# Routed attention with an ELU network: conversion order, query masks on ScalarE, row sums of ten blocks on TensorE, weight sums on VectorE

## The chip, the core and the metric

The kernel runs on one core of a Trainium2 chip. A core has TensorE (matrix products, PE in the profile; PEld is its loading of weights), VectorE (DVE), ScalarE (ACT), GpSimd (POOL) and a queue for transfers (SP). The metric is the time of the core on the device in microseconds, the median of several runs.

## The reference, cut to what matters

Attention over 4 batches, 8 heads, 768 positions of 64 values each. Queries and keys are each assigned to the nearest of 16 centroids of their head, and a query sees only the keys of its own centroid. The result goes through a two-layer network with an ELU between.

```python
q_assign = np.argmax(np.einsum('bhsd,hcd->bhsc', q_n, c_n), axis=-1)
k_assign = np.argmax(np.einsum('bhsd,hcd->bhsc', k_n, c_n), axis=-1)
mask = q_assign[:, :, :, None] == k_assign[:, :, None, :]
scores = scale * np.matmul(q, k.transpose(0, 1, 3, 2))
scores = np.where(mask, scores, -1000000000.0)
attn = softmax(scores)                      # written out in the reference
attn_out = np.matmul(attn, v)
# ... (B,H,S,D) -> x of (B*S, H*D) = 3072 x 512
h = x @ w_in                                # 512 x 2048
g = np.where(h > 0.0, h, np.exp(np.minimum(h, 0.0)) - 1.0)
out = g @ w_out                             # 2048 x 512
```

The two weight matrices arrive as 64-bit floating point numbers, everything else in 32 bits.

## The kernel before

**Converting the weights.** 32 pieces of 128x512 weights are brought in as pairs of 32-bit words (low, high) and turned into 32-bit numbers. A step handles three pieces in different states. "Splitting" takes the mantissa bits and the exponent bits out of the high word; in between, ScalarE rebuilds the exponent and GpSimd scales the mantissa; "joining" adds sign and low word, and GpSimd multiplies the two parts. The tile `ex` has three buffers.

```python
for n in range(len(pieces) + 2) if wide else ():
    if n < len(pieces):                                   # split piece n
        high = words[n][0][:, :, 1]
        e = exps[n] = loads.tile([P, WC], U32, name="ex", tag="ex", bufs=3)
        nc.vector.tensor_scalar(                                            # L244
            pieces[n][0].bitcast(U32), high, 0xFFFFF, None, op0=Alu.bitwise_and)
        nc.vector.tensor_scalar(e, high, 0x7FF00000, None, op0=Alu.bitwise_and)  # L247
    if 0 <= n - 1 < len(pieces):                          # convert piece n - 1
        to, ex = pieces[n - 1][0], exps[n - 1]
        nc.scalar.activation(ex, ex, Act.Relu, scale=8.0, bias=off)         # L250
        nc.gpsimd.tensor_scalar(                                            # L251
            to, to.bitcast(U32), 2.0**-20, 1.0, op0=Alu.mult, op1=Alu.add)
    if n > 1:                                             # join piece n - 2
        to, ex = pieces[n - 2][0], exps.pop(n - 2)
        w, place, limit = words.pop(n - 2)
        nc.vector.scalar_tensor_tensor(                                     # L257
            ex, w[:, :, 1], 0x80000000, ex, op0=Alu.bitwise_and, op1=Alu.bitwise_or)
        nc.vector.scalar_tensor_tensor(                                     # L260
            to, w[:, :, 0], 2.0**-52, to, op0=Alu.mult, op1=Alu.add)
        nc.gpsimd.tensor_tensor(to, to, ex.bitcast(F32), op=Alu.mult)       # L263
        places.append((place, limit))
        ask()                                             # load the next words
    yield
```

`weigh(k)` runs k of these steps. There are three in each of the first ten attention blocks, and one beside each step of the network until the ninth block.

**An attention block** is one pair of heads and a third (256) of the queries; there are 48, twelve to a batch. Scores of block n are made in three tiles of PSUM, each from products of q and k (L401) and, added to them, products of two small masks (L410), of which `qm` is the queries' one. It holds 0 where a query belongs to a centroid and -2^80 elsewhere; the exponential of that is 0.

```python
def masks(n):
    b, third, pr = blocks[n]
    qm[n] = route.tile([P, QS], BF16, name="qm", tag="qm", bufs=2)
    for e in range(2):
        rows = slice(64 * e, 64 * e + 64)
        m = big[rows, pr % 2 : pr % 2 + 1]
        nc.vector.tensor_scalar(                                            # L374
            qm[n][rows], hot[b, 0][rows, side(pr, e), ts(third, QS)],
            m, m, op0=Alu.mult, op1=Alu.subtract)

def scores(n):
    for u in range(NT // 2):              # three tiles
        s = banks()                       # one of three pairs of PSUM banks
        # ... products L401 and L410 into s
        p = pu[n, u] = probs.tile([P, 2, 2 * QS], F32, name="p", tag="p")
        nc.scalar.activation(p, s, Act.Exp, scale=SCALE)                    # L418
        if n < LAG + 3:                   # LAG = 7
            weigh(1)
```

The sums of the rows of `p` are a product with ones (L436) on TensorE. Where `sums` has run, VectorE has added the parts first, and 4 small matmul instructions are left of 24.

```python
def sums(n):
    to = osum[n] = work.tile([P, 2, 2 * QS], F32, name="psum", tag="psum", bufs=1)
    nc.vector.tensor_tensor(to, pu[n, 0], pu[n, 1], op=Alu.add)             # L424
    nc.vector.tensor_tensor(to, to, pu[n, 2], op=Alu.add)                   # L425
    nc.vector.tensor_tensor(to[:, :, :QS], to[:, :, :QS], to[:, :, QS:], op=Alu.add)  # L426

def values(n):
    # ... products of p and v into o_bank (L447); row sums into d (L436)
    nc.scalar.copy(x, o_bank[:, :QS])                                       # L461
    nc.scalar.activation(r, d[:, :QS], Act.Copy, accum_out=...)             # L463
    nc.vector.reciprocal(r, r)                                              # L464
    nc.gpsimd.tensor_tensor(x, x, r, op=Alu.mult)                           # L465
```

`check(n)` reads r once more on ScalarE (L471).

**The network** runs seven blocks behind, on a third of a batch's rows, in groups of steps: two hidden steps; two more; four products; three products. A hidden step is 32 products (L486, 64 instructions) into a bank pair, an exponential (ScalarE, L496), a clamp (GpSimd, L497), and one step later `elu` (VectorE, L503, then a difference, L505 or L507), which frees the bank pair. The products of the second layer (L516) use fewer multiplications by working with sums of `g` and of the weights. Those of the weights are made once, in two halves, after the last conversion:

```python
def sum_weights(half):
    of = slice(half * FC // 4, (half + 1) * FC // 4)
    e_, f_, g_, h_ = (x[:, of] for x in w_parts())     # views of w_out
    t1, t2, t4 = (w_sum[:, n, of] for n in range(3))
    nc.gpsimd.tensor_tensor(t1, f_, e_, op=Alu.subtract)                    # L295
    nc.gpsimd.tensor_tensor(f_, h_, f_, op=Alu.subtract)                    # L296
    nc.vector.tensor_tensor(t2, h_, t1, op=Alu.subtract)                    # L297
    nc.vector.tensor_tensor(t4, g_, t2, op=Alu.subtract)                    # L298
```

In the second layer `first` multiplies e_, `second` g_, `third_` the changed f_, `fourth` t4.

**The order of a block's iteration** (cut):

```python
for n in range(len(blocks) + LAG):
    if n <= len(blocks) and n > 0:
        values(n - 1)
    # ... loads of q, k, v
    if n + 1 < len(blocks) and at + 1 < NB:      # not the last block of a batch
        masks(n + 1)
    if n < len(blocks):
        scores(n)
    if 0 < n <= len(blocks):
        check(n - 1)
    if n < len(blocks):
        if n >= LAG:
            sums(n)
        # ... in the last four blocks of a batch: transposes of the next q, k (VectorE, L310)
    # in the last block of a batch, beside the network's steps: similarities (TensorE, L331)
    # and assignment (VectorE, L338 to L363) of the next queries, then of the next keys,
    # then masks(n + 1)
    if n == LAG + 2:
        weigh(100)
        for half in range(2):
            sum_weights(half)
    # the network's group n - LAG, step by step; one weigh(1) after each where n < LAG + 2
```

At the start the queries are transposed (ScalarE copies qT out of PSUM, L323), assigned, then `masks(0)`, and then the same for the keys (kT).

Of the kernel before, what the change touches and what calls it, by code (L numbers as in the profile page):

```python
# [9 lines left out]
F32 = mybir.dt.float32  # L10
# [3 lines left out]
Act = mybir.ActivationFunctionType  # L14
Alu = mybir.AluOpType
# [3 lines left out]
P = 128  # L19


BIG = float(2.0**80)
# [38 lines left out]
def main_path(ctx, tc, c, q, k, v, centroids, moe_w_in, moe_w_out, out):  # L61
    nc = tc.nc
# [16 lines left out]
    const = ctx.enter_context(tc.tile_pool(name="const", bufs=1))  # L79
# [81 lines left out]
    big = const.tile([P, 2], F32, name="big")  # L161
    for e in range(2):
        rows = slice(64 * e, 64 * e + 64)
        nc.vector.tensor_reduce(
            big[rows],
            ident[rows].rearrange("q (h x e c) -> q x e h c", h=2, x=2, e=2)[:, :, e],
            axis=Axis.XY,
            op=Alu.add,
        )
    nc.vector.tensor_scalar(big, big, BIG, None, op0=Alu.mult)  # L170

    sq = work.tile([P, D], F32, name="sq", tag="r", bufs=1)
# [15 lines left out]
    for e in range(2):  # L188
# [17 lines left out]
    pieces = [  # L206
        (w_in[:, ch, ts(g, WC)], moe_w_in[ts(ch, P), ts(g, WC)])
        for g in range(DF // WC)
        for ch in range(KC)
    ]  # L210
# [4 lines left out]
    words, exps = {}, {}  # L215
    places = []
    asked = 0

    def ask():

        nonlocal asked
        while asked < len(pieces):
            to, src = pieces[asked]
            if not wide:
                nc.sync.dma_start(to, src)
                asked += 1
                continue
            places[:] = [x for x in places if asked < x[1]]
            if not places:
                return  # L230
            place, limit = places.pop(0)
            w = place.bitcast(U32)
            nc.sync.dma_start(w, src.bitcast(U32))
            words[asked] = (w.rearrange("p (n w) -> p n w", w=2), place, limit)
            asked += 1

    def weight_steps():


        for n in range(len(pieces) + 2) if wide else ():  # L240
            if n < len(pieces):
                high = words[n][0][:, :, 1]
                e = exps[n] = loads.tile([P, WC], U32, name="ex", tag="ex", bufs=3)
                nc.vector.tensor_scalar(  # L244
                    pieces[n][0].bitcast(U32), high, 0xFFFFF, None, op0=Alu.bitwise_and
                )
                nc.vector.tensor_scalar(e, high, 0x7FF00000, None, op0=Alu.bitwise_and)  # L247
            if 0 <= n - 1 < len(pieces):
                to, ex = pieces[n - 1][0], exps[n - 1]
                nc.scalar.activation(ex, ex, Act.Relu, scale=8.0, bias=off)  # L250
                nc.gpsimd.tensor_scalar(  # L251
                    to, to.bitcast(U32), 2.0**-20, 1.0, op0=Alu.mult, op1=Alu.add
                )
            if n > 1:
                to, ex = pieces[n - 2][0], exps.pop(n - 2)
                w, place, limit = words.pop(n - 2)
                nc.vector.scalar_tensor_tensor(  # L257
                    ex, w[:, :, 1], 0x80000000, ex, op0=Alu.bitwise_and, op1=Alu.bitwise_or
                )
                nc.vector.scalar_tensor_tensor(  # L260
                    to, w[:, :, 0], 2.0**-52, to, op0=Alu.mult, op1=Alu.add
                )
                nc.gpsimd.tensor_tensor(to, to, ex.bitcast(F32), op=Alu.mult)  # L263
                places.append((place, limit))
                ask()
            yield

    spare = w_sum.rearrange("p a f m -> p (a f m)")
# [16 lines left out]
    def w_parts():  # L285
        e_, f_ = w_out[:, : FC // 2, :QS], w_out[:, : FC // 2, QS:]
        g_, h_ = w_out[:, FC // 2 :, :QS], w_out[:, FC // 2 :, QS:]
        return e_, f_, g_, h_

    def sum_weights(half):  # L290

        of = slice(half * FC // 4, (half + 1) * FC // 4)
        e_, f_, g_, h_ = (x[:, of] for x in w_parts())
        t1, t2, t4 = (w_sum[:, n, of] for n in range(3))
        nc.gpsimd.tensor_tensor(t1, f_, e_, op=Alu.subtract)  # L295
        nc.gpsimd.tensor_tensor(f_, h_, f_, op=Alu.subtract)  # L296
        nc.vector.tensor_tensor(t2, h_, t1, op=Alu.subtract)  # L297
        nc.vector.tensor_tensor(t4, g_, t2, op=Alu.subtract)  # L298
# [66 lines left out]
    def side(pr, e):  # L365
        return int(pr // 2 != e)
# [4 lines that stand above are left out]
        for e in range(2):  # L371
            rows = slice(64 * e, 64 * e + 64)
            m = big[rows, pr % 2 : pr % 2 + 1]
            nc.vector.tensor_scalar(  # L374
                qm[n][rows],
                hot[b, 0][rows, side(pr, e), ts(third, QS)],
                m,
                m,
                op0=Alu.mult,
                op1=Alu.subtract,  # L380
            )


    LAG = 7
# [43 lines left out]
    def values(n):  # L428

        b, third, pr = blocks[n]  # L430
        d = banks()[:, 0]
        summed = osum.pop(n, None)

        def row_sums(p, m, kt, last):
            for e in range(2):
                nc.tensor.matmul(  # L436
                    d[64 * e : 64 * e + 64, :QS],
                    lhsT=ones,
                    rhs=p[:, e, ts(m, QS)],
                    start=(kt == 0),  # L440
                    stop=(kt == last),
                )

        for kt in range(NT):
            p, m = pu[n, kt // 2], kt % 2
            for e in range(2):
                nc.tensor.matmul(  # L447
                    o_bank[64 * e : 64 * e + 64, :QS],
                    lhsT=raw["v", n][:, e, kt],
                    rhs=p[:, e, ts(m, QS)],  # L450
                    start=(kt == 0),
                    stop=(kt == NT - 1),
                )
            if summed is None:
                row_sums(p, m, kt, NT - 1)
        if summed is not None:
            row_sums(summed, 0, 0, 0)
        if pr == 0:
            xT[b, third] = xtp.tile([P, KC, QS], F32, name="xT", tag="xT")
        x = xT[b, third][:, pr]  # L460
        nc.scalar.copy(x, o_bank[:, :QS])  # L461
        r = work.tile([P, QS], F32, name="r", tag="r", bufs=1)
        nc.scalar.activation(r, d[:, :QS], Act.Copy, accum_out=d_sum[:, n : n + 1])  # L463
        nc.vector.reciprocal(r, r)  # L464
        nc.gpsimd.tensor_tensor(x, x, r, op=Alu.mult)  # L465
        rs[n] = r
# [154 lines left out]
    for n in range(len(blocks) + LAG):  # L621
        b, at = n // NB, n % NB
        ahead = b + 1 < B
        if n <= len(blocks) and n > 0:
            values(n - 1)
        if ahead:
            for pr in {5: [0], 6: [1], 9: [2], 10: [3]}.get(at, []):
                load("q", (b + 1) * NPR + pr)
                load("k", (b + 1) * NPR + pr)
        if n + 1 < len(blocks):  # L630
            load_v(n + 1)
        if n + 1 < len(blocks) and at + 1 < NB:
# [3 lines that stand above are left out]
        if 0 < n <= len(blocks):  # L636
            check(n - 1)
        if n < len(blocks):
            if n >= LAG:
                sums(n)  # L640
            if ahead and at in turns:
                for j in range(2):
                    turn((b + 1) * NPR + turns[at], j)
        beside = []
        if ahead and at + 1 == NB:
            beside.append(None)
            for j in range(2):
                beside.append(lambda b=b, j=j: [similar(b + 1, j, half) for half in range(2)])
                beside.append(lambda b=b, j=j: [assign(b + 1, j, half) for half in range(2)])
            beside.append(lambda n=n: masks(n + 1))  # L650
        main = groups[n - LAG] if n >= LAG else []
# [4 lines that stand above are left out]
        done = 0  # L656
        for m, step in enumerate(main):
            step()
            upto = len(beside) * (m + 1) // len(main)
            for other in beside[done:upto]:  # L660
                if other:
                    other()
            done = upto
            if n < LAG + 2:
                weigh(1)
        for other in beside[done:]:
            if other:
                other()
# [268 lines left out]
```

## Time and profile before

| | |
|---|---|
| Median of 3 runs | 1068.94 us (1066.64 to 1069.65) |
| Span of the profiled execution | 1066.4 us, clock 0.976 |
| Length of a block early on (45.67 to 57.73 us) | 12.06 us |
| Iterations 7, 8 and 9, from reciprocal to reciprocal | 105.99 to 130.22, to 161.74; the fourth product of the network ends at 191.9 us |
| Stage after that | 187 us to the end |
| Busy time of VectorE, ScalarE, GpSimd | 559.3, 293.8, 188.9 us |

The profile gives for each group of instructions its line in the kernel, its engine, what it writes and reads, its count, busy time and mean duration. Rows of a timeline start with the start time and the duration in us; a bracket at the end holds the idle time of the engine before the instruction and what ended it. Rows of waits give the waiting instruction, what it waited for, the total in us, how often, and the longest.

### The profile page before, as it was taken

The page shows a single profiled execution, that of the slowest core. Times are in us where ns is not written, and L with a number is a line of the kernel's source. Part 1 is how long each engine was busy: PE and PEld are TensorE (multiplying, and loading weights), DVE is VectorE, ACT ScalarE, POOL GpSimd, SP SyncE. Part 2 cuts the span into 40 slices and gives each one's busy share as a digit, 9 for nine tenths or more (in the row PEclk, how much of TensorE's full clock was granted, in tenths as well). Part 3 has the DMA queues.
Part 4 walks back from the last instruction along what each step waited for, and adds up shares of the span by engine and source line. Part 5 has one row for each costly group of instructions (what it writes and reads, how often), then busy time and mean ns, then how long its engine had stood idle before and what let it go on. Part 6 is the DMA issues. An engine that isn't in the chain of part 4 may idle for free.

```text
span 1066.4 us, 14860 instructions
## 1 busy us (share of the span) xinstructions
PE 1011.3 (95%) x6343; PEld 784.4 (74%) x6343; DVE 559.3 (52%) x740; ACT 293.8 (28%) x499; POOL 188.9 (18%) x195
## 2 busy tenths in 40 slices
PE   6988876999999999999999999999999999999996
PEld 4655654767877878877887887876787787788885
DVE  5778999476336336465534535656444534533131
ACT  3555331223123133122223223222322322321010
POOL 0555657011011011011011011011011011011010
PEclk9999886999999999999999999999999999999999
DMA  9628231100015012210013212210010000000000
GB/s 298 255 75 212 81 84 30 38 28 16 16 46 78 15 50 45 45 36 29 18 36 62 42 35 60 45 35 16 30 35 15 31 35 15 31 21 1 20 1 23
DMA packets 103961, 55.60 MB, mean 52 GB/s; under 512 B 83408, under 2 KB 96720, under 8 KB 103888
## 3 DMA queue, kind: packets, MB, share of 16 engines
q1 hardware_dynamic: 103888, 54.57, 18.8%
q8 instruction: 52, 0.85, 0.3%
q14 instruction: 21, 0.17, 0.0%
HBM read 48.27 MB, written 6.29 MB: 51 GB/s over the span
## 4 chain that ended last, share of the span: by engine, by line
PE 82%; DVE 13%; POOL 4%; issue 1%; DMA 0%; ACT 0%; DVEq 0%; POOLq 0%
PE banks L486 29%; PE f_bank L516 16%; PE o_bank L516 12%; PE banks L401 10%; PE o_bank L447 10%; PE banks L410 3%; DVE ex L257 2%; PE banks L436 2%; DVE r L464 1%; POOL w_in L263 1%; POOL w_out L263 1%; DVE ex L247 1%; DVE qm L374 1%; DVE w_in L260 1%; DVE w_out L260 1%; PE banks L331 1%
## 5 line engine op out<-in xcount | busy, mean ns | idle before, releaser
L486 PE MATMUL banks<-xT,w_in 128*128 128x256 f32 x1536 | 338.4, 381 | 0.3
L486 PEld LDWEIGHTS banks<-xT,w_in 128*128 128x128 f32 x1536 | 289.8, 190 | 47.8 <-ACT p L418 2.9
L401 PE MATMUL banks<-qT,kT 64*128 64x256 f32 x1152 | 174.5, 401 | 8.5 <-DVE gT L503 8.3
L418 ACT ACTIVATE p<-banks 128x1024 f32<-128x1024 f32 x144 | 147.3, 1023 | 58.6 <-PE banks L410 54.2
L447 PE MATMUL o_bank<-p,v_raw 128*64 128x256 f32 x1152 | 143.1, 387 | 11.6 <-ACT p L418 11.2
L464 DVE RECIPROCAL r<-r 128x256 f32<-128x256 f32 x48 | 84.0, 1749 | 113.7 <-ACT r L463 113.6
L503 DVE SCALAR_TENSOR_TENSOR gT<-gT,banks 128x1024 f32<-128x1024 f32 x48 | 58.4, 1216 | 156.8 <-POOL gT L497 156.7
L401 PEld LDWEIGHTS banks<-qT,kT 64*128 64x128 f32 x1152 | 91.7, 195 | 60.1 <-issue 11.3
L496 ACT ACTIVATE gT<-banks 128x1024 f32<-128x1024 f32 x48 | 49.1, 1024 | 280.9 <-PE banks L486 280.9
L447 PEld LDWEIGHTS o_bank<-p,v_raw 128*64 128x64 f32 x1152 | 78.9, 138 | 64.8 <-issue 17.2
L497 POOL TENSOR_SCALAR gT<-gT 128x1024 f32<-128x1024 f32 x48 | 52.8, 1100 | 320.0 <-ACT gT L496 320.0
L516 PE MATMUL o_bank<-w_out,gT 128*128 128x256 f32 x384 | 91.8, 393 | 8.1 <-POOL w_out L296 8.1
L465 POOL TENSOR_TENSOR xT<-xT,r 128x256 f32<-128x256 f32 x48 | 35.0, 729 | 318.7 <-DVE r L464 318.7
L410 PE MATMUL banks<-qm,hot 64*128 64x256 bf16 x576 | 82.9, 276 | 8.6 <-DVE qm L374 5.4
L516 PEld LDWEIGHTS o_bank<-w_out,gT 128*128 128x128 f32 x384 | 74.1, 196 | 22.5 <-POOL w_out L296 9.2
L516 PE MATMUL f_bank<-w_out,gT 128*128 128x256 f32 x384 | 87.1, 379 | 1.3 <-POOL w_out L263 1.3
L516 PEld LDWEIGHTS f_bank<-w_out,gT 128*128 128x128 f32 x384 | 72.9, 190 | 11.6 <-POOL w_out L263 1.7
L461 ACT COPY xT<-o_bank 128x256 f32<-128x256 f32 x48 | 17.8, 370 | 218.5 <-PE o_bank L447 218.4
L424 DVE TENSOR_TENSOR psum<-p 128x1024 f32<-128x1024 f32 x41 | 50.2, 1224 | 13.0 <-ACT p L418 12.7
L425 DVE TENSOR_TENSOR psum<-psum,p 128x1024 f32<-128x1024 f32 x41 | 52.9, 1290 | 5.0 <-ACT p L418 1.6
L516 PE MATMUL f_bank<-w_sum,g_sum 128*128 128x256 f32 x192 | 44.6, 386 | 1.2 <-DVE part L563 1.2
L374 DVE TENSOR_SCALAR qm<-hot,big 64x256 bf16<-64x256 bf16 x96 | 45.2, 470 | 1.0
(108 smaller groups left out, 829.2 us busy)
## 6 DMA issues: line engine op xcount, KB each, us to landing
v_raw<-in_v_dram SPq DMA_DIRECT2D x48, 384.0 KB, 3.2
w_sum<-in_moe_w_out_dram SPq DMA_DIRECT2D x12, 512.0 KB, 4.2
out_dram<-o_sb SPq DMA_DIRECT2D x24, 256.0 KB, 2.0
q_raw<-in_q_dram SPq DMA_DIRECT2D x48, 96.0 KB, 3.6
k_raw<-in_k_dram SPq DMA_DIRECT2D x48, 96.0 KB, 3.2
w_sum<-in_moe_w_in_dram SPq DMA_DIRECT2D x8, 512.0 KB, 6.6
w_out<-in_moe_w_in_dram SPq DMA_DIRECT2D x8, 512.0 KB, 10.4
w_out<-in_moe_w_out_dram SPq DMA_DIRECT2D x4, 512.0 KB, 4.3
```

Source lines behind the costliest of these rows:

```text
L374: nc.vector.tensor_scalar(qm[n][rows], hot[b, 0][rows, side(pr, e), ts(third, QS)], m, m, op0=Alu.mult, op1=Alu.subtract,)
L401: nc.tensor.matmul(s[:, e, ts(m, QS)], lhsT=T[i, 1][rows, ts(kt, P)], rhs=T[i, 0][rows, cols], start=True, stop=False,)
L410: nc.tensor.matmul(s[:, e, ts(m, QS)], lhsT=hot[b, 1][rows, side(pr, e), ts(kt, P)], rhs=qm[n][rows], start=False, stop=True,)
L418: nc.scalar.activation(p, s, Act.Exp, scale=SCALE)
L424: nc.vector.tensor_tensor(to, pu[n, 0], pu[n, 1], op=Alu.add)
L425: nc.vector.tensor_tensor(to, to, pu[n, 2], op=Alu.add)
L447: nc.tensor.matmul(o_bank[64 * e : 64 * e + 64, :QS], lhsT=raw["v", n][:, e, kt], rhs=p[:, e, ts(m, QS)], start=(kt == 0), stop=(kt == NT ...
L464: nc.vector.reciprocal(r, r)
L486: nc.tensor.matmul(hf[:, f], lhsT=w_in[:, ch, ts(4 * n + f, P)], rhs=xT[b, third][:, ch], start=(ch == 0 and f % 2 == 0), stop=(ch == KC - 1),
L497: nc.gpsimd.tensor_scalar(t, t, 1.0, 0.0, op0=Alu.min, op1=Alu.max)
L503: nc.vector.scalar_tensor_tensor(t, t, -1.0, hf, op0=Alu.add, op1=Alu.max)
L516: nc.tensor.matmul(to[:, :QS], lhsT=left[:, f], rhs=right[:, f], start=(f == 0), stop=(f == FC // 2 - 1),)
```

## The change

The conversion steps join piece n - 2 before they split piece n, so that the wait of the split for a buffer comes later. The masks of queries are made by ScalarE, as big * hot - big, with a new constant `minus`. In blocks 7, 8 and 9 VectorE no longer adds the parts of p, so TensorE sums the rows of ten blocks alone. Of the four sums of weights, three are on VectorE and one on GpSimd.

```diff
+    minus = const.tile([P, 2], F32, name="minus")
+    nc.vector.tensor_scalar(minus, big, -BIG, None, op0=Alu.mult)
     nc.vector.tensor_scalar(big, big, BIG, None, op0=Alu.mult)
...
         for n in range(len(pieces) + 2) if wide else ():
+            if n > 1:
+                # join piece n - 2: L257, L260, L263 and ask(), as before
             if n < len(pieces):
                 # split piece n
...
                 # convert piece n - 1
-            if n > 1:
-                # join piece n - 2
             yield
...
-        nc.gpsimd.tensor_tensor(t1, f_, e_, op=Alu.subtract)
+        nc.vector.tensor_tensor(t1, f_, e_, op=Alu.subtract)
...
-            nc.vector.tensor_scalar(
+            nc.scalar.activation(
                 qm[n][rows],
                 hot[b, 0][rows, side(pr, e), ts(third, QS)],
-                m,
-                m,
-                op0=Alu.mult,
-                op1=Alu.subtract,
+                Act.Identity,
+                scale=m,
+                bias=minus[rows, pr % 2 : pr % 2 + 1],
             )
...
-            if n >= LAG:
+            if n >= LAG + 3:
                 sums(n)
```

More of the change, by code (lines that the diff above doesn't have):

```diff
@@ L240, in weight_steps @@
         for n in range(len(pieces) + 2) if wide else ():
+            if n > 1:
+                to, ex = pieces[n - 2][0], exps.pop(n - 2)
+                w, place, limit = words.pop(n - 2)
+                nc.vector.scalar_tensor_tensor(
+                    ex, w[:, :, 1], 0x80000000, ex, op0=Alu.bitwise_and, op1=Alu.bitwise_or
+                )
+                nc.vector.scalar_tensor_tensor(
+                    to, w[:, :, 0], 2.0**-52, to, op0=Alu.mult, op1=Alu.add
+                )
+                nc.gpsimd.tensor_tensor(to, to, ex.bitcast(F32), op=Alu.mult)
+                places.append((place, limit))
+                ask()
             if n < len(pieces):
@@ L253, in weight_steps @@
                 )
-            if n > 1:
[L255 to L265, printed above, removed]
             yield
```

## The prediction

> **What bounds the kernel now.** I read the engine shares first. TensorE looks like the bound, but an average over 1066 us hides stages, so the second view was the table of windows, cut where the program changes (columns: length, then busy us and instructions of PE, PEld, DVE, ACT, POOL, then the granted clock and DMA).
>
> ```profile
> PE 1011.3 (95%) x6343; PEld 784.4 (74%) x6343; DVE 559.3 (52%) x740; ACT 293.8 (28%) x499; POOL 188.9 (18%) x195
> ```
>
> ```profile
> core 0: us, PE busy (x) PEld busy (x) DVE busy (x) ACT busy (x) POOL busy (x), PEclk, DMA share, GB/s
> 45.67:57.73 12.06, 10.12 (x98) 6.44 (x98) 9.67 (x16) 6.35 (x12) 7.09 (x7) 1.00 0.56 187
> 161.74:187.19 25.45, 15.99 (x59) 11.38 (x54) 25.21 (x20) 2.55 (x5) 18.90 (x9) 0.70 0.20 31
> 187.19:430.00 242.81, 240.72 (x1511) 187.86 (x1512) 123.37 (x154) 66.31 (x114) 25.62 (x30) 1.00 0.17 38
> ```
>
> There are two stages. Up to about 190 us the chain of waits runs through VectorE and GpSimd (DVE 13% and POOL 4% of the span are this stage); after it, TensorE is busy 240.72 of 242.81 us. All four parts of the change aim at VectorE, so they can pay only in the first 190 us, or where a wait for VectorE is left in the second.
>
> In the first stage one attention block takes 12.06 us. Its timeline, VectorE then GpSimd:
>
> ```profile
> 45.67 1.74 DVE L464 RECIPROCAL r<-r 128x256 f32<-128x256 f32 x1
> ...
> 50.05 0.68 DVE L260 SCALAR_TENSOR_TENSOR w_in<-w_sum,w_in 128x512 f32<-128x512 uint32 x1
> 50.65 0.41 DVE L244 TENSOR_SCALAR w_in<-w_out 128x512 uint32<-128x512 uint32 x1
> 52.23 0.43 DVE L247 TENSOR_SCALAR ex<-w_out 128x512 uint32<-128x512 uint32 x1 [1.16 <-POOL w_in L263]
> 52.57 1.10 DVE L257 SCALAR_TENSOR_TENSOR ex<-w_sum,ex 128x512 uint32<-128x512 uint32 x1
> 53.59 0.68 DVE L260 SCALAR_TENSOR_TENSOR w_in<-w_sum,w_in 128x512 f32<-128x512 uint32 x1
> ```
>
> ```profile
> 45.83 1.28 POOL L263 TENSOR_TENSOR w_in<-w_in,ex 128x512 f32<-128x512 f32 x1 [1.22 <-DVE w_in L260]
> ...
> 50.81 1.38 POOL L263 TENSOR_TENSOR w_in<-w_in,ex 128x512 f32<-128x512 f32 x1 [1.89 <-DVE w_in L260]
> 52.28 0.85 POOL L251 TENSOR_SCALAR w_in<-w_in 128x512 f32<-128x512 uint32 x1
> ```
>
> The split L247 waits 1.16 us for GpSimd's product L263. But look at what runs together: L251 takes 0.85 us beside VectorE work and 0.62 alone (48.30 us), L257 takes 1.10 beside L251 and 0.68 alone (49.45 us), while the reciprocal (1.74) and the product under it (1.28) do not slow each other.
>
> **What the Trainium skill says.** "SBUF — State Buffer", section "Who interferes with whom": GpSimd shares a port pair with VectorE as an exclusive lock, and a VectorE operation takes part if it has two SBUF inputs or runs in a two-port mode; the loser blocks. The trace agrees, also on who is next:
>
> ```profile
> 166.12 0.68 DVE L257 SCALAR_TENSOR_TENSOR ex<-w_sum,ex 128x512 uint32<-128x512 uint32 x1
> 166.72 1.75 DVE L260 SCALAR_TENSOR_TENSOR w_out<-w_sum,w_out 128x512 f32<-128x512 uint32 x1
> ```
>
> ```profile
> 166.28 1.65 POOL L263 TENSOR_TENSOR w_out<-w_out,ex 128x512 f32<-128x512 f32 x1 [1.22 <-DVE w_out L260]
> ```
>
> The product, issued during L257, went in between L257 and L260, which then took 1.75 instead of 0.68. So a waiting engine gets the pair when the running instruction ends, and the two alternate. "ScalarE: Activation LUTs", section "What ACT_TABLE_LOAD costs", gives 93 ns for each per-partition operand; its section "Table sets: the hidden batching unit" has identity in every set, so I expect no new table load (no run shows it yet). "TensorE: Matmul & The Clock Gate", section "What's actually happening", has an idle TensorE fall to half clock; here the granted clock is 0.70 in the window with the gaps.
>
> **Join first.** Within a steady step (L260 at 50.05 to L260 at 53.59, 3.54 us) six instructions follow one another, L244, L263, L247, L251, L257, L260, all users of the shared pair, and 3.54 is about the sum of their holds. The new order runs the same cycle, cut at another place: L247 no longer waits for the buffer, but finds the pair taken by the same product. So the 18.6 us of L247's waits (11.6 on w_in and 7.0 on w_out) are not a gain. What the cut does change is which GpSimd operation lies under the reciprocal, the one long VectorE operation outside the lock: before, the product (1.28); after, the cheaper conversion L251 (0.55). That loses 0.7 us a block.
>
> **Masks on ScalarE.** VectorE loses two operations, 0.96 us a block (47.33 to 48.29), part of it beside xT's product L465. The new segment from the last split to the next join: L244 to L247's end 1.87, reciprocal 1.66, L257 0.60, L465 0.62 (it waits for the reciprocal and gets in between), L260 0.60: 5.35 us. The old one, L260 to L260 across the reciprocal (45.67 to 50.65): 4.98. With two steady steps, 5.35 + 7.08 = 12.4 against 12.06: **+0.3 us** a block, six blocks: +1.8.
>
> On ScalarE one mask should take 0.60 us: a 256-column activation without such operands takes 406 ns (L471), plus two times 0.1, which the row of L250 confirms (721 ns for 512 columns with one operand, at 0.85 ns a column from L461 and L418). Two of them, overlapping by 0.1: 1.1 us. In the first stage ScalarE is busy 6.35 of 12.06 us, so it has room. At the start masks(0) now stands before the copies of kT: hot for its columns is there at 17.1 us, the copies start near 17.7 instead of 15.6, and VectorE's first transpose of the keys' similarities moves from 20.7 to 21.4: **+0.7 us**.
>
> In the second stage two waits are concerned.
>
> ```profile
> DVE ex L247 <- POOL w_in L263: 11.6, 10, 1.2
> ```
>
> ```profile
> PE banks L410 <- DVE qm L374: 5.4, 3, 1.8
> ```
>
> At each of three changes of batch TensorE waits 1.8 us for masks that VectorE makes last, after the keys' assignment. ScalarE needs only the queries' assignment, done some 9 us earlier (hot at 229.5, masks at 238.2), so this wait goes; some 1.95 us each with the bank wait after it: **-5.9 us**. Against it, after the first two hidden steps of a third one bank is still held, and the third score tile waits for the first exponential:
>
> ```profile
> 318.28 0.19 ACT L463 ACTIVATION_READ_ACCUMULATOR r<-banks 128x1 f32 x1
> 319.22 2.11 ACT L418 ACTIVATE p<-banks 128x1024 f32<-128x1024 f32 x2 [0.74 <-PE banks L410]
> ```
>
> ```profile
> 320.29 0.70 PE L401 MATMUL banks<-qT,kT 64*128 64x256 f32 x4
> ```
>
> ScalarE's gap of 0.74 us does not hold 1.1 us of masks; the exponential starts 0.3 later, in six blocks (16, 20, 28, 32, 40, 44): **+1.8 us**. Elsewhere a third bank is free and 0.3 us is hidden.
>
> **TensorE sums rows of ten blocks.** Blocks 7 to 9 lose three additions on VectorE (L424 to L426: 4.8, 4.8 and 6.1 us in the timeline, about 2.95 of it their own, the rest waiting for GpSimd). TensorE does 24 small matmuls instead of 4: values took 5.3 us in block 0 (27.68 to 33.0) and 3.2 in block 9 (191.86 to 195.03), so +2.1 us each. For blocks 7 and 8 TensorE has gaps; block 9's come at 192 us, where TensorE is the bound: **+2.1 us**.
>
> **Sums of weights.** GpSimd's L295 takes 3.3 us twice; on VectorE an addition of 128x1024 takes 1.23.
>
> I lay out blocks 7 to 9 with these durations, alternating the lock. Block 7, reciprocal to reciprocal: 12.4 (as above) + 4.55 (a step with the clamp L497, 1.0, inside) + 2.25 (L503, which is outside the lock, a rest of L497, L505) + 3.07 (a step whose L251 lay under L503) = 22.3 against 24.2: **-1.9**. Block 8: 12.4 + 1.85 (two transposes) + three times 1.8 (L503 with L505 or L507) + 0.4 + 3 times 3.07 = 29.3 against 31.5: **-2.2**. Block 9: joins to 6.5, last product on GpSimd to 7.9, transposes to 8.4, first t1 to 9.5, t2 before GpSimd's f_ to 10.7, f_ to 13.3, t4, t1 to 15.5, t2 to 16.7, second f_ to 19.3, t4 to 20.4. Third product resumes at 19.3 instead of 21.6; the fourth ends at 27.8 instead of 30.2: **-2.4**.
>
> The sum: 0.7 + 1.8 - 1.9 - 2.2 - 2.4 = -4.0 up to the start of the TensorE stage; with +2.1 - 5.9 + 1.8 in it, **-6.0 us**, so 1063.
>
> **Rivals.** (a) The wait of L247 really goes, and VectorE becomes the bound of the block: 9.67 busy less 0.96 of masks is 8.7 us, and TensorE's own block is 8.8 (scores 3.46, from 53.12 to 56.58; values 5.3, from 27.68 to 33.0). Then seven blocks gain 3.3 us each: about 1040. For it: the row of waits. Against it: L257 at 1.10 and L260 at 1.75 us, which only a lock explains. (b) ScalarE becomes the pacer: it is in order, and its masks stand before the exponentials that free the banks. If the masks took 1.6 us, or every block felt 0.3 us, the second stage would lose 10 us more: 1073. Against it: a third bank is free in three blocks of four. (c) The batch wait stays because the keys' assignment ends as late as the masks did (hot at 238.16): then -1 instead of -5.9, and 1068. Against it: the first half of the keys' columns is there at 235.8, and TensorE needs the second half only with the fourth key tile.
>
> **Range and chances.** Each of the eight terms is within some 2 us, and (b) and (c) lean to the slow side, (a) in part to the fast: 1055 to 1070 holds it 8 times in 10. For 2% either way it takes 1047.6 or 1090.3; only all of (a) reaches the first, and nothing I see the second: faster 0.04, same 0.94, slower 0.02.
>
> **What would show it.** A block in the early stage at 12.1 to 12.6 us, with L247 at 1.5 us or more behind L263 in place of its wait; masks near 0.60 us each on ScalarE; the qm row gone from the waits of TensorE; the TensorE stage starting some 4 us earlier; its later blocks as long as before but for 0.3 us in one of four. An early block under 11.5 us would refute the lock argument, and make the prediction too slow.

## The result and the profile after

The changed kernel takes 1054.32 us (median, 1053.14 to 1055.71) against 1069.3 before: ratio 0.9865, 95% interval 0.9843 to 0.9886. That is 15 us faster, where 6 were predicted, and just below the predicted range. The engine shares and three windows like those of before (same columns: length, then busy us and instructions of PE, PEld, DVE, ACT, POOL, then clock and DMA; the second ends here with the network's fourth product, before with its third):

```profile
PE 1009.7 (96%) x6403; PEld 785.7 (75%) x6403; DVE 531.3 (51%) x638; ACT 343.2 (33%) x595; POOL 182.2 (17%) x193
```

```profile
35.98:47.82 11.84, 11.38 (x114) 7.53 (x112) 11.84 (x13) 8.50 (x16) 6.68 (x7) 1.00 0.45 138
...
155.27:181.40 26.13, 18.27 (x66) 13.85 (x68) 20.44 (x17) 3.80 (x7) 13.14 (x8) 0.80 0.20 31
181.40:430.00 248.60, 247.18 (x1576) 193.04 (x1578) 112.75 (x130) 79.42 (x142) 26.54 (x30) 1.00 0.17 39
```

An early block is 11.84 us long, and VectorE is busy in all of it; before, it was 12.06 with 9.67 busy. VectorE lost two operations and is busier: its waits have become longer operations. The timeline says which. The line numbers have moved: L258 and L261 are the split (L244 and L247 before), L246 and L249 the join (L257 and L260), L252 the product (L263), L265 the conversion (L251), L466 xT's product.

```profile
47.82 1.74 DVE L465 RECIPROCAL r<-r 128x256 f32<-128x256 f32 x1
...
53.93 0.68 DVE L249 SCALAR_TENSOR_TENSOR w_in<-w_sum,w_in 128x512 f32<-128x512 uint32 x1
54.53 0.41 DVE L258 TENSOR_SCALAR w_in<-w_out 128x512 uint32<-128x512 uint32 x1
54.87 1.49 DVE L261 TENSOR_SCALAR ex<-w_out 128x512 uint32<-128x512 uint32 x1
56.28 1.09 DVE L246 SCALAR_TENSOR_TENSOR ex<-w_out,ex 128x512 uint32<-128x512 uint32 x1
```

GpSimd in the same stretch:

```profile
47.70 0.68 POOL L265 TENSOR_SCALAR w_in<-w_in 128x512 f32<-128x512 uint32 x1
49.65 1.04 POOL L466 TENSOR_TENSOR xT<-xT,r 128x256 f32<-128x256 f32 x1 [1.27 <-DVE r L465]
...
54.69 1.39 POOL L252 TENSOR_TENSOR w_in<-w_in,ex 128x512 f32<-128x512 f32 x1 [1.22 <-DVE w_in L249]
```

L261 has no wait any more, and takes 1.49 us instead of 0.43: it stands behind the product at the shared port pair. Under the reciprocal at 47.82 lies the conversion (0.68), no longer the product.

Where the time came from, stage by stage, from the timelines and chains of the two profiles:

| Stage | before | after | measured | predicted |
|---|---|---|---|---|
| to the first reciprocal | 33.56 | 35.98 | +2.4 | +0.7 |
| six blocks | 72.43 | 70.94 | -1.5 | +1.8 |
| block 7 | 24.23 | 21.14 | -3.1 | -1.9 |
| block 8 | 31.52 | 27.21 | -4.3 | -2.2 |
| block 9, to the end of the fourth product | 30.19 | 26.1 | -4.1 | -2.4 |
| values of block 9, to the fifth product | 6.63 | 8.79 | +2.2 | +2.1 |
| three changes of batch | 82.2 | 74.0 | -8.2 | -5.9 |
| six blocks with a wait for ScalarE | 6.93 each | 7.31 each | +2.3 | +1.8 |
| sum | | | -14.3 | -6.0 |

The first row can't be laid to the change: in profiles of kernels with the old start the first reciprocal stands at 33.56, 34.80, 35.32 and 35.42 us, and the profile before, with the 33.56, is that of the fastest execution (1066.64 us). About 2 us of the rows of blocks 7 and 8 can't be laid to it either: two later runs with the same code up to there took 22.12 and 22.13 us in block 7, and one of them 28.31 in block 8 (last section).

### The profile page after: what moved, and what is told of

Same layout as the page of the kernel before. It is cut to its first block, busy times and chain, and to the rows that moved or that the text cites. A ratio compares the mean times of both kernels' runs of the same rounds, so it can differ in the third digit from the quotient of the medians.

```text
span 1051.9 us, 14992 instructions
## 1 busy us (share of the span) xinstructions
PE 1009.7 (96%) x6403; PEld 785.7 (75%) x6403; DVE 531.3 (51%) x638; ACT 343.2 (33%) x595; POOL 182.2 (17%) x193
## 4 chain that ended last, share of the span: by engine, by line
PE 82%; DVE 14%; ACT 2%; issue 1%; POOL 1%; DMA 0%; ACTq 0%; DVEq 0%; POOLq 0%
PE banks L487 29%; PE f_bank L517 16%; PE o_bank L517 12%; PE o_bank L448 10%; PE banks L402 9%; DVE ex L261 4%; DVE ex L246 2%; PE banks L437 2%; PE banks L411 2%; DVE r L465 1%; DVE w_out L249 1%; DVE w_in L249 1%; ACT qm L376 1%; PE banks L333 1%; ACT p L419 1%; PE banks L322 1%
## 5 line engine op out<-in xcount | busy, mean ns | idle before, releaser
L402 PE MATMUL banks<-qT,kT 64*128 64x256 f32 x1152 | 168.2, 392 | 4.9 <-ACT p L419 4.4
L419 ACT ACTIVATE p<-banks 128x1024 f32<-128x1024 f32 x144 | 140.6, 1022 | 13.3 <-PE banks L411 11.8
L402 PEld LDWEIGHTS banks<-qT,kT 64*128 64x128 f32 x1152 | 88.7, 189 | 55.2 <-PE o_bank L448 11.1
L498 POOL TENSOR_SCALAR gT<-gT 128x1024 f32<-128x1024 f32 x48 | 50.2, 1046 | 313.3 <-ACT gT L497 313.0
L466 POOL TENSOR_TENSOR xT<-xT,r 128x256 f32<-128x256 f32 x48 | 40.7, 847 | 324.5 <-DVE r L465 324.4
L411 PE MATMUL banks<-qm,hot 64*128 64x256 bf16 x576 | 80.5, 271 | 2.0 <-DVE hot L362 2.0
L425 DVE TENSOR_TENSOR psum<-p 128x1024 f32<-128x1024 f32 x38 | 46.6, 1226 | 42.2 <-ACT p L419 42.2
L376 ACT ACTIVATE qm<-hot,minus,big 64x256 bf16<-64x256 bf16 x96 | 56.7, 591 | 4.1 <-DVE hot L362 3.3
L426 DVE TENSOR_TENSOR psum<-psum,p 128x1024 f32<-128x1024 f32 x38 | 46.9, 1235 | 6.0 <-ACT p L419 3.0
```

What stands on the lines that cost most here:

```text
L376: nc.scalar.activation(qm[n][rows], hot[b, 0][rows, side(pr, e), ts(third, QS)], Act.Identity, scale=m, bias=minus[rows, pr % 2 : pr % 2 + 1],
L402: nc.tensor.matmul(s[:, e, ts(m, QS)], lhsT=T[i, 1][rows, ts(kt, P)], rhs=T[i, 0][rows, cols], start=True, stop=False,)
L411: nc.tensor.matmul(s[:, e, ts(m, QS)], lhsT=hot[b, 1][rows, side(pr, e), ts(kt, P)], rhs=qm[n][rows], start=False, stop=True,)
L498: nc.gpsimd.tensor_scalar(t, t, 1.0, 0.0, op0=Alu.min, op1=Alu.max)
```

## The experiments

Theory 1 is the prediction's: the shared pair paces the first stage, TensorE's own waits the second. Its rival (theory 2) is the change's own idea, that the split's buffer wait was the cost. All ratios are to the kernel before, timed beside each run.

**Each part alone, on the kernel before.** Only the join first:

```diff
 for n in range(len(pieces) + 2) if wide else ():
+    if n > 1:          # join piece n - 2
     if n < len(pieces):    # split piece n
     ...
-    if n > 1:          # join piece n - 2
```

> The kernel before with the join moved ahead of the split, nothing else. If the shared port pair paces the conversion (theory 1), the wait of the split for its buffer (18.6 us in 16 waits) turns into a split that takes about 1.5 us behind the product, and only some 0.17 us of signalling goes at each; against that the cheaper conversion lies under the reciprocal instead of the product, +0.4 to +0.7 us in each of nine blocks. Sum: 0 to +3 us. If the buffer wait was the cost (theory 2): 12 to 18 us faster.

Measured: 1073.68 us, ratio 1.0039 (1.0026 to 1.0053), 4 us slower; an early block takes 12.37 us instead of 12.06. The wait is gone from the split, and the kernel is slower. Theory 2 falls.

Only the masks on ScalarE:

```diff
-            nc.vector.tensor_scalar(qm[n][rows], ..., m, m, op0=Alu.mult, op1=Alu.subtract)
+            nc.scalar.activation(qm[n][rows], ..., Act.Identity, scale=m, bias=minus[...])
```

> The kernel before with the masks on ScalarE, nothing else. Theory 1: VectorE loses 0.7 to 0.96 us in nine blocks (-6 to -8), the three changes of batch lose their waits and the half clock that follows two of them (26.5, 27.9 and 27.9 us to 24.7: -8.2), six blocks wait 0.38 for the exponential (+2.3), the start +0.9: -12 us in all. Rival: the batch changes bring only their waits, 1.8 each, and ScalarE's queue costs in every block: -2 to -5 us.

Measured: 1058.36 us, 0.9895 (0.988 to 0.991), 11 us faster; early blocks of 11.52 us, batch changes of 24.65. As theory 1 had it.

Only the row sums of blocks 7 to 9 on TensorE:

```diff
-            if n >= LAG:
+            if n >= LAG + 3:
                 sums(n)
```

> The kernel before without VectorE's additions in blocks 7, 8 and 9. Theory 1: their own 2.95 us and most of the waiting beside them go, 3 to 4.3 us a block, and block 9 pays 2.16 us of TensorE: -7 to -10 us. Rival: the additions ran where VectorE and GpSimd waited anyway: -2 us or nothing.

Measured: 1061.7 us, 0.9925 (0.9911 to 0.9938), 8 us faster, within the expectation.

Only the first sum of weights on VectorE:

```diff
-        nc.gpsimd.tensor_tensor(t1, f_, e_, op=Alu.subtract)
+        nc.vector.tensor_tensor(t1, f_, e_, op=Alu.subtract)
```

> The kernel before with the first sum of weights on VectorE. Theory 1: alone it is of no use, because GpSimd began it at 170.7 us under VectorE's additions, and VectorE comes to it only after them and two transposes, at 176 us: 2 to 5 us slower. Rival: 5 us of GpSimd's time less on the path: 2 to 4 us faster.

Measured: 1069.83 us, 1.0002 (0.9993 to 1.001): the same, and both expectations were wrong. VectorE does come late to this sum (175.5 us). What I had missed is that GpSimd, left idle, no longer holds the pair against VectorE's last addition of block 9. That addition before, and in this run:

```profile
171.85 2.71 DVE L426 TENSOR_TENSOR psum<-psum 128x512 f32<-128x512 f32 x1
```

```profile
173.11 0.69 DVE L426 TENSOR_TENSOR psum<-psum 128x512 f32<-128x512 f32 x1
```

The 2 us saved there more than pay for the later start: from the reciprocal of block 9's iteration to the next, this profile has 32.97 us and the one before 33.98. But its first change of batch takes 27.83 us instead of 26.49, and the times show no gain. The four parts alone add up to +4.2 - 11.1 - 7.8 + 0.4 = -14.3 us; together they give -15.

**Is it the buffer or the pair?** The old order, but five buffers for the exponent words, so that no split waits for one:

```diff
-                e = exps[n] = loads.tile([P, WC], U32, name="ex", tag="ex", bufs=3)
+                if n % 5 > 2:
+                    e = work.tile([P, DM], U32, name="ex2", tag="o_sb")
+                else:
+                    e = loads.tile([P, WC], U32, name="ex", tag="ex", bufs=3)
+                exps[n] = e
```

> The kernel before in its old order, with five buffers for the exponent words instead of three (two of them the tiles of the output, which are free then), so that the split waits for no buffer. Theory 1 (shared pair): the split is held 1.5 us at the pair in place of its 1.16 us wait and 0.43, the step goes from 3.54 to 3.37, 16 times: -2.7 us. Theory 2 (buffer): the 18.6 us of waits go, block 12.06 to about 9.7: -15 us or more.

Measured: 1066.82 us, 0.9977 (0.9967 to 0.9986): 2.8 us faster, as theory 1 gave it; an early block takes 11.72 us. The split in this run (L248 and L251 are its two operations here):

```profile
62.29 0.41 DVE L248 TENSOR_SCALAR w_in<-w_out 128x512 uint32<-128x512 uint32 x1
62.63 1.49 DVE L251 TENSOR_SCALAR ex<-w_out 128x512 uint32<-128x512 uint32 x1
64.04 1.09 DVE L261 SCALAR_TENSOR_TENSOR ex<-w_out,ex 128x512 uint32<-128x512 uint32 x1
```

With the buffer free the second split takes 1.49 us. The step went from 3.54 to 3.37 us: 0.17 us is all that the buffer wait cost over the wait at the pair.

**The change without the join first:**

```diff
-    if n > 1:          # join piece n - 2, ahead of the split
...
+    if n > 1:          # join piece n - 2, as in the kernel before
```

> The changed kernel with split ahead of join again. Theory 1: the wait comes back (+0.17 us in 16 steps), and the product lies under the reciprocal again (-0.5 us in nine blocks): within 3 us of the changed kernel, block about 11.8 us. Theory 2: 10 us or more slower than the changed kernel.

Measured: 1050.74 us, 0.9824 (0.9806 to 0.9842); early blocks of 11.52 us instead of 11.82. The interval ends just below that of the changed kernel (0.9843 to 0.9886); with the 4 us of the run with the join alone, and the same 0.31 us a block in both pairs, this part of the change costs about 4 us.

**What a change of batch was waiting for.** The kernel before, with the masks of the next batch's first block between the queries' and the keys' assignment, still on VectorE:

```diff
             for j in range(2):
                 beside.append(...similar...)
                 beside.append(...assign...)
+                if j == 0:
+                    beside.append(lambda n=n: masks(n + 1))
-            beside.append(lambda n=n: masks(n + 1))
```

> The kernel before, masks on VectorE, but for the first block of the next batch they stand between the queries' and the keys' assignment. If the order is what counts at a change of batch, TensorE's 1.8 us waits and the half clock after them go: the three changes take 24.7 to 25.0 us instead of 26.5, 27.9, 27.9: -7 to -8 us, without ScalarE. If it is VectorE's load: within 1 us of before.

Measured: 1058.54 us, 0.9899 (0.9883 to 0.9914), 11 us faster. A change of batch takes 24.14 us, shorter than the 24.65 of the changed kernel, as no mask stands in front of an exponential: 82.2 - 3 times 24.14 = 9.8 us. One line in another place, without ScalarE, brings as much as the whole move of the masks. TensorE at the second change of batch, before:

```profile
482.35 0.69 PE L410 MATMUL banks<-qm,hot 64*128 64x256 bf16 x2 [1.79 <-DVE qm L374]
482.74 1.17 PE L401 MATMUL banks<-qT,kT 64*128 64x256 f32 x4
...
484.97 1.07 PE L401 MATMUL banks<-qT,kT 64*128 64x256 f32 x4
```

and in this run:

```profile
478.66 0.28 PE L410 MATMUL banks<-qm,hot 64*128 64x256 bf16 x2
478.77 0.60 PE L401 MATMUL banks<-qT,kT 64*128 64x256 f32 x4
```

After the 1.79 us of waiting, four matmuls take 1.07 us instead of 0.60 for some 3 us more (the granted clock from 483 to 486 us is 0.50). That is why the second and third change took 27.86 us and the first 26.49.

**Masks behind the exponentials.** In the changed kernel, masks(n + 1) after scores(n), and masks(0) after the keys' copies:

```diff
-        if j == 0:             # at the start
+        if j == 1:
             masks(0)
...
-        if n + 1 < len(blocks) and at + 1 < NB:
-            masks(n + 1)
         if n < len(blocks):
             scores(n)
+        if n + 1 < len(blocks) and at + 1 < NB:
+            masks(n + 1)
```

> The changed kernel, with the masks of block n + 1 issued after the exponentials of block n, and the first masks after the copies of the first keys. If the masks in front of the exponential cost the 0.38 us that six blocks show, those go, and 0.9 us at the start: 3 us faster than the changed kernel. If ScalarE's order does not matter: the same as the changed kernel.

Measured: 1050.11 us, 0.9825 (0.9807 to 0.9842), 4 us faster than the changed kernel. TensorE's waits for this exponential after 190 us are gone. There were nine in the changed kernel, in six blocks and three changes of batch (its whole profile has ten):

```profile
PE banks L402 <- ACT p L419: 4.4, 10, 0.5
```

At the second change of batch of the changed kernel, ScalarE and then TensorE:

```profile
471.04 1.19 ACT L376 ACTIVATE qm<-hot,minus,big 64x256 bf16<-64x256 bf16 x2
472.26 1.94 ACT L419 ACTIVATE p<-banks 128x1024 f32<-128x1024 f32 x2
```

```profile
473.34 0.70 PE L402 MATMUL banks<-qT,kT 64*128 64x256 f32 x4 [0.53 <-ACT p L419]
```

Without them the six blocks are back at 6.93 us (2.3 us together), and a change of batch takes 24.15 us instead of 24.65 (1.5 us for three). The expectation had left out the changes of batch, and the 0.9 us that it gave to the start can't be told from the differences of the starts.

**What the move to ScalarE itself is worth.** The changed kernel with the masks on VectorE again, in the early place at a change of batch (with `minus` gone too):

```diff
-            nc.scalar.activation(qm[n][rows], ..., Act.Identity, scale=m, bias=minus[...])
+            nc.vector.tensor_scalar(qm[n][rows], ..., m, m, op0=Alu.mult, op1=Alu.subtract)
...
+                if j == 0:
+                    beside.append(lambda n=n: masks(n + 1))
-            beside.append(lambda n=n: masks(n + 1))
```

> The changed kernel with the masks back on VectorE, at a change of batch between the queries' and the keys' assignment. Theory 1: early blocks of 12.4 us instead of 11.8, +5 us over nine; the batch changes 0.5 us shorter each and six blocks 0.38 shorter, as no mask stands in front of an exponential, -3.8: 1 us slower than the changed kernel. If the move to ScalarE were what the change lives on: 10 us slower.

Measured: 1055.68 us, 0.9867 (0.9852 to 0.9882), as the changed kernel within its interval; early blocks of 12.37 us. With the order put right, VectorE's 0.55 us in the early blocks and ScalarE's waits in the late ones cancel, unless the masks stand behind the exponentials.

**The sum of weights, with the row sums gone.** The changed kernel with t1 on GpSimd:

```diff
-        nc.vector.tensor_tensor(t1, f_, e_, op=Alu.subtract)
+        nc.gpsimd.tensor_tensor(t1, f_, e_, op=Alu.subtract)
```

> The changed kernel with the first sum of weights on GpSimd again. With VectorE's additions of blocks 7 to 9 gone, VectorE stands idle where GpSimd makes this sum (1.9 and 2.2 us in the run with the row sums alone), so here, and only here, it is worth having on VectorE: 2 us slower than the changed kernel. If it is worth as little as it was alone: the same within 1 us.

Measured: 1057.49 us, 0.9878 (0.9863 to 0.9893), 3 us slower than the changed kernel by the medians, though the intervals overlap. By the profiles 1.5 us of it lie in block 9 (33.55 us instead of 32.04 between the reciprocals); 2.1 lie in blocks 7 and 8, ahead of the edit, and are no effect of it. What block 9 waits for is seen in the run with the row sums alone, in which VectorE waits for GpSimd's sum twice:

```profile
166.59 1.23 DVE L297 TENSOR_TENSOR w_sum<-w_out,w_sum 128x1024 f32<-128x1024 f32 x1 [1.94 <-POOL w_sum L295]
...
173.33 1.23 DVE L297 TENSOR_TENSOR w_sum<-w_out,w_sum 128x1024 f32<-128x1024 f32 x1 [2.23 <-POOL w_sum L295]
```

So the times show nothing of this part alone; beside the row sums the profiles show some 1.5 us.

**Block 9 given back to VectorE**, in the changed kernel:

```diff
-            if n >= LAG + 3:
+            if n >= LAG + 2:
                 sums(n)
```

> The changed kernel with VectorE's additions back in block 9 alone. TensorE gets 2.1 us back in a place where it is the bound, VectorE and GpSimd get 3 to 5 us more in front of the sums of weights, on which TensorE's third and fourth product wait: 1 to 3 us slower than the changed kernel. If TensorE's row sums were the dearer: 1 to 2 us faster.

Measured: 1056.16 us, 0.9867 (0.9852 to 0.9883): 1.8 us more by the medians, not clear of the changed kernel. In the profile block 9 takes 34.93 us between the reciprocals instead of 32.04, TensorE's row sums included, so its 2.2 us for block 9 are at least not a mistake.

**What the experiments point to.** The changed kernel with split ahead of join, five exponent buffers, and the masks behind the exponentials:

```diff
-    if n > 1:          # join piece n - 2, ahead of the split
+                if n % 5 > 2:    # ex from the output's tiles, as in the run above
+    if n > 1:          # join piece n - 2, after split and conversion
...
-            masks(n + 1)       # ahead of scores(n)
+            masks(n + 1)       # after scores(n); masks(0) after the keys
```

> The changed kernel with what the earlier runs favoured: split ahead of join (-3.6 us against the changed kernel), masks after the exponentials and the first ones after the keys' copies (-4.2), five exponent buffers (-2.7 in the old kernel: two waits of 0.17 a block). If the three are independent, as the shared pair has it: 10 us faster than the changed kernel, about 1044 us, with early blocks of 11.2 us. If they share a cause: 5 us, about 1049.

Measured: 1040.68 us, 0.9725 (0.9712 to 0.9739): 29 us faster than before and 13.6 faster than the change. Early blocks of 11.17 us. The reciprocal on VectorE, and the product that again lies under it on GpSimd, neither slowed:

```profile
44.89 1.74 DVE L469 RECIPROCAL r<-r 128x256 f32<-128x256 f32 x1
```

```profile
45.05 1.27 POOL L269 TENSOR_TENSOR w_in<-w_in,ex 128x512 f32<-128x512 f32 x1 [1.22 <-DVE w_in L266]
```

The three edits do not take from one another: against the 13.6 us, the medians of the single runs would have given 3.6 + 4.2 + 2.8 = 10.6 us.

## Why the prediction was wrong, step by step

**The bound and the mechanism were right.** The first stage is paced by the pair, and the join first costs more than it brings. "The Trainium skill", page "SBUF — State Buffer", section "Who interferes with whom", says that the loser blocks for the whole instruction; the trace agrees: the second operation of the split takes 1.49 us behind the product, in the changed kernel and in the run with five buffers, and 0.43 where it had waited before. Rival (a) is refuted by the run with five buffers (a block of 11.72 us, not 8.7), rival (b) by masks of 0.59 us that hold TensorE up in six blocks and three changes of batch only, rival (c) by the row of qm, which is gone from TensorE's waits.

Of the 8.3 us between the sums, the layout of blocks 7 to 9 is 5.0, the early blocks 3.3 and the changes of batch 2.3; the start (1.7) and two small rows (0.6) go the other way.

**The step of "+0.3 us a block" failed**, with the wrong sign (-0.25). I carried the step of 3.54 us over as it was ("The new order runs the same cycle"). Here the wait by semaphore costs 0.17 us a step more than the same wait at the pair, as the run with five buffers shows alone; and the segment across the reciprocal took 5.10 us, not 5.35. 5.10 + 2 times 3.37 = 11.84. The runs split it: join first +0.31, masks -0.55. The loss of 0.7 us under the reciprocal, forecast for the join, was about right: 0.31 and two steps of 0.17 make 0.65.

**The layout of blocks 7 to 9 was 5 us too small.** In block 7 five steps of 0.17 would explain 0.85 of 1.2 us; but this block's 21.14 us are partly luck, as the profiles of two other runs with the same code have 22.1, close to the predicted 22.3, and there TensorE, which the layout left out, is busy all the time (last section). In block 8 six steps explain 1.0 of 2.1; nearly all of the rest is one product that did not get between the two splits and so lay under the reciprocal (below). In block 9 I kept the products' durations of a TensorE at clock 0.71; it ran at 0.80, and the resumed third product took 2.75 instead of 3.78 us, the fourth 4.47 instead of 4.74: 1.3 of 1.7 us.

**The change of batch was mis-sized by 2.3 us**: the wait and the bank wait after it were counted (1.95 us; the first change, without half clock, lost 1.84), the half clock that follows in two of three cases was not, though the length of the three changes (26.5, 27.9, 27.9) stood in the chain of the profile before.

**Right in size**: block 9's row sums (+2.2 for +2.1), the mask on ScalarE (0.59 us for 0.60), the wait in six blocks (0.38 for 0.3). The page "ScalarE: Activation LUTs", section "Table sets: the hidden batching unit", has identity in every set; the trace has two table loads, as before.

**Left open**: the start. Its +0.7 us can't be told from the 1.9 us by which profiles of one and the same start differ.

## What to carry to other kernels

A wait in the trace is worth only what ends after it: before removing a wait of VectorE for GpSimd, look whether the same operation would then stand behind the same GpSimd instruction at the shared pair. Put the longest GpSimd operation under the one VectorE operation that does not use the pair, and in a queue of one engine put work that is wanted late behind the work that frees a buffer. Where TensorE is the bound, follow each of its waits past its end: the clock after it may cost as much again.

## What was not expected of the hardware

After a single wait of 1.8 us TensorE ran at half rate for 3 us: four matmuls in 1.07 instead of 0.60 us, in two of three changes of batch before, in one of three in the run with the row sums alone, in all three in that with the first sum of weights alone, and in none of the changed kernel, where no such wait is left.

The same thing makes block 7 differ in profiles of the same code. In block 6 of the changed kernel TensorE waits 2.50 us for an exponential and goes on at full rate (clock of the block 1.00). In the run with t1 on GpSimd it waits 2.52 us at the same place, four matmuls then take up to 1.07 us instead of 0.60 (clock 0.86), and the network's 64 matmuls start at 109.00 instead of 107.77 us, though the block's reciprocal came no later. Block 7 then takes 22.12 us with TensorE busy in all of it, instead of 21.14. The run with block 9 on VectorE has the same clock of 0.86 there and 22.13 us.

The pair does not always alternate. At the end of block 8 of the changed kernel the product came during the first split and yet ran behind the second; VectorE and then GpSimd:

```profile
154.60 0.44 DVE L258 TENSOR_SCALAR w_out<-w_sum 128x512 uint32<-128x512 uint32 x1
154.93 0.44 DVE L261 TENSOR_SCALAR ex<-w_sum 128x512 uint32<-128x512 uint32 x1
```

```profile
154.77 1.75 POOL L252 TENSOR_TENSOR w_out<-w_out,ex 128x512 f32<-128x512 f32 x1 [2.67 <-DVE w_out L249]
```

The same happened at that place in the run with block 9 on VectorE, and not in those with t1 on GpSimd or the masks behind the exponentials, where L261 took 1.50 and 1.49 us. What decides it, no run shows.
